# Pairing input spectra with adding transfers instead of pairing kernel spectra on VectorE, in a four-layer S4 and SwiGLU kernel

## The chip, the cores and the metric

The program runs on one core of a Trainium2 chip. The metric is device time in microseconds (us) of one execution, from outside the profile; the profile has its own, slightly shorter span from first to last instruction. Engines are named as in the profile: PE is TensorE (PEld its weight loads), DVE is VectorE, ACT is ScalarE, POOL is GpSimd, SP is SyncE, which here only issues DMAs.

## What is computed

The input is a sequence of 2048 rows of 512 channels. Two layers follow one another, each an S4 convolution and a SwiGLU feed-forward network (FFN), each behind a layer norm and with a residual:

```python
def _A_ref(u, A_re, A_im, B_re, B_im, C_re, C_im, log_dt, Dskip):
    ...
    P = jnp.exp(logdA[:, :, None] * l[None, None, :])
    K = jnp.einsum("dn,dnl,dn->dl", Cc, P, dB).real
    ...
    Yf = Uf * Kf[None, :, :, :]
    ...
    y = (lambda x, *d: x.transpose(*d))(y, 0, 2, 1) + u * Dskip[None, None, :]
    return y
...
x = x + _A_ref(_layernorm(x, axis=-1), A_A_re, A_A_im, A_B_re, A_B_im, A_C_re, A_C_im, A_log_dt, A_Dskip)
x = x + _B_ref(_layernorm(x, axis=-1), B_w_gate, B_w_up, B_w_down)
```

So per channel a kernel K of 2048 lags is built from 128 complex modes, the input is convolved with it causally, and the direct term u times Dskip is added. Both layers use the same parameters, so K is built once.

## The kernel before

**Blocks.** The sequence is cut into four blocks of 512 rows. A block of inputs and a block of lags are transformed by a discrete Fourier transform (DFT) of length 1024 at odd half frequencies, written as matmuls with cosine and sine tables (`ef`, `ek`), in four parts q and two halves h of 256 channels. An output block b is the inverse transform of the sum over k of (input spectrum of block b-k) times (spectrum W of lag block k). A product of two blocks of 512 spreads over 1024 outputs, so the second half of each product belongs to the next block. Before, this is put into the kernel spectra: W of block k is the transform of lag block k plus that of lag block k-1 with real and imaginary parts swapped and a sign, which shifts it by 512.

**Generation (to about 270 us).** K is built in eight chunks of 64 channels. Per chunk: `gen_turns` (DVE, angles as integer turns by doubling), `gen_trig` (ACT, sine and cosine) and `gen_exp` (ACT, exponentials) fill `re` and `im`, the large factor for lags that are multiples of 32; `gen_e` (DVE, L428 to L441) multiplies phase and size; `gen_g` (DVE, L443 to L476) builds `g`, the small factor for lags 0 to 31, by doubling. For the last doubling of chunks 1 to 6 one product is added by an accumulating DMA that POOL issues (L465). `lags` (L478) makes all lags of the 64 channels: per channel four small matmuls, two with `re` and two with `im` as the moving operand (f32 matmuls appear as two instructions), with the channels of a group of 16 on one of four 32-column strips of TensorE, so that four run beside each other. Before, `re` is laid out as 65 lags by 64 channels, so a matmul for one channel reads every 64th element. `spread_in` and `spread` (two DMA trips through DRAM) or `spread_pe` turn the lags into `kt`, and `spectra` (L526) transforms them: matmuls in `products` (L515) into PSUM tile `pw`, among them a matmul of one row that adds Dskip to all frequencies (L517), two ACT copies with a sign and swapped parts (L542), one ACT copy of block 0 into the resident `w0r` (L543), one DVE add (L545), and two stores into the DRAM array `wdr`. `later_parts` (L563) and `first_parts` (L551) do the same for the last two chunks, after the loop.

**Order in generation.** It is written out by hand: `manual_schedule` keeps program order on ACT, DVE and PE (and on SP inside the loop). Steps are put into a list `plan` with a due time each (`at(t, step)`, L986), chunk c starting at `starts[c]`, 28 units apart from chunk 3 on. The list is sorted and executed; the due times set only the order, the chip sets the pace. In the loop chunk i is in `use` (lags and spectra), chunk i+1 in `factors` (`gen_g`, `gen_e`), chunk i+2 in `prepare` (angles and exponentials). Between them run `second_block` (forward transform of input block 1 by `direct`, L283) and the sums of squares of the FFN weights (`norms`).

**The rest.** Eight pairs of (layer, block) follow in the order `SEQ` (L44). `ssm_half` (L716) computes a convolution: per q it loads W of block k and the older input spectra `uu` from DRAM (arrays `wdr`, `udr`), multiplies on DVE (L754), adds (L757), and transforms back (L773). The newest spectrum `u` comes from `forward` (L242; DVE butterflies, PE matmuls L273, ACT copy L275), one q ahead of its use, and is stored to `udr` by a POOL DMA (L706). `ffn` (L869) has the large matmuls (L886 to L903). Here the scheduler of the framework orders the engines, with a priority boost on some stretches. Tiles share a few buffers by tag: `uu` has three, `u` two, `w` three, `t1` three.

Of the kernel before, what the change touches and what calls it, by code (L numbers as in the profile page):

```python
# [22 lines left out]
P = 128  # L23
# [50 lines left out]
def kernel(ctx, tc, x, a_re, a_im, b_re, b_im, c_re, c_im, log_dt, d_skip,  # L74
# [65 lines left out]
    one = sb.tile([P, 1], F32, name="one")  # L140
    G.memset(one, 1.0)
# [4 lines left out]
    udr = [dram.tile([NB - 1, 2, 4, P, 2, HD], F32, name=f"udr{i}") for i in range(NL)]  # L146
    xdr = dram.tile([NB, 4, P, D], F32, name="xdr")
# [94 lines left out]
    def forward(n, h, eh):  # L242
# [13 lines left out]
        for i, q in enumerate(QORD):  # L256
# [4 lines left out]
            if eh:  # L261
                hl = z2[:, 1].bitcast(F16).rearrange("p i (l d) -> p l i d", l=2)
                A.activation(hl[:, 0], z, AF.Copy, scale=256.0)
                stt(hl[:, 1], z, 256.0, hl[:, 0], OP.subtract)
            pf = psml([P, 2, HD], "pf")
            with tc.high_priority(offset=BOOST):
# [7 lines left out]
                u = tl([P, 2, HD], "u", "u")  # L274
                A.activation(u, pf, AF.Copy, scale=2.0 ** -16 if eh else 1.0)  # L275
# [7 lines left out]
    def direct(b, h, q, n, space=psml):  # L283
# [9 lines left out]
        nc.sync.dma_start(udr[0][b, h, q], u)  # L293
# [58 lines left out]
    def gen_tiles(ch):  # L352
        re = tl([P, 65, DC], "re", f"W{2 * (ch % 2)}")
        im = tl([P, 65, DC], "im", f"W{2 * (ch % 2) + 1}")
        mu = tl([P, 32, DC], "mu", "n")
        xz = tl([P, 3, 5, DC], "xz", "bd")
        mz = mz2[:, ch % 2]
        return re, im, mu, xz, mz


# [14 lines left out]
    def gen_turns(ch, ts):  # L375

        re, im, mu, xz, mz = ts
# [3 lines left out]
        tu = im[:, 33:65].bitcast(I32)  # L381
# [3 lines left out]
        for n in (2, 4, 8, 16):  # L385
            V.tensor_tensor(tu[:, n:2 * n], tu[:, 0:n], tu[:, n - 1:n].to_broadcast([P, n, DC]), OP.add)
            yield
        G.memset(im[:, 32], 0.0)
        yield

    def gen_trig(ts):


        re, im, mu, xz, mz = ts
        A.activation(xz[:, 2], xz[:, 1].bitcast(I32), AF.Sin, scale=-TWO_PI / TURN)
        for c, s in ((xz[:, 0], xz[:, 1]), (re[:, 33:65], im[:, 33:65])):
            turns = s.bitcast(I32)
            A.activation(c, turns, AF.Abs)
            A.activation(s, turns, AF.Sin, scale=TWO_PI / TURN)
            A.activation(c, c, AF.Sin, scale=-TWO_PI / TURN, bias=hpi)  # L400
            yield

    def gen_exp(ch, ts):


        re, im, mu, xz, mz = ts
# [4 lines left out]
        G.memset(re[:, 0], 1.0)  # L411
        for a in sorted(LOW):
            A.activation(re[:, a], r_, AF.Exp, scale=32.0 * a)
# [3 lines left out]
    def upper(ts):  # L417

        A.activation(ts[2][:, 1:], ts[0][:, 1:32], AF.Square)

    def squares(ts):

        re = ts[0]
        for st in (2, 4):
            A.activation(re[:, st:33:2 * st], re[:, st // 2:17:st], AF.Square)
            yield

    def gen_e(ts):  # L428
# [3 lines left out]
        half = [[t.rearrange("p a (g h d) -> p a g h d", g=4, h=2)[:, :, :, o] for t in (re, mu)] for o in range(2)]  # L432
        V.tensor_tensor(im[:, :32], im[:, 64:32:-1], re[:, :32], OP.mult)
# [802 lines left out]
```

## Time and profile before

| what | value |
|---|---|
| time, median of 3 runs | 1186.87 us (1183.84 to 1190.97) |
| the profiled execution's own time | 1186.51 us |
| its span | 1184.7 us |
| instructions in the span | 24523 |
| ACT busy | 587.1 us (50%) |
| POOL busy | 92.2 us (8%) |
| moved by DMA | 151.17 MB, mean 128 GB/s |
| mean granted TensorE clock | 0.991 |

Busy times are unions over an engine's instructions. Matmuls are pipelined and last longer in the trace than they occupy the array, so a PE at 100% has no gap longer than a pipeline's depth, which does not by itself make it the limit. The profile's lists of groups give for each source line its engine, operation, shape, count, total busy time, mean ns of one, and the idle time of the engine just before with what ended it. The chain is followed back from the last instruction.

### The profile page before, as it was taken

The page shows a single profiled execution, that of the slowest core. Times are in us where ns is not written, and L with a number is a line of the kernel's source. Part 1 is how long each engine was busy: PE and PEld are TensorE (multiplying, and loading weights), DVE is VectorE, ACT ScalarE, POOL GpSimd, SP SyncE. Part 2 cuts the span into 40 slices and gives each one's busy share as a digit, 9 for nine tenths or more (in the row PEclk, how much of TensorE's full clock was granted, in tenths as well). Part 3 has the DMA queues.
Part 4 walks back from the last instruction along what each step waited for, and adds up shares of the span by engine and source line. Part 5 has one row for each costly group of instructions (what it writes and reads, how often), then busy time and mean ns, then how long its engine had stood idle before and what let it go on. Part 6 is the DMA issues. An engine that isn't in the chain of part 4 may idle for free.

```text
span 1184.7 us, 24523 instructions
## 1 busy us (share of the span) xinstructions
PE 1117.3 (94%) x10008; PEld 884.8 (75%) x10008; DVE 1006.2 (85%) x1591; ACT 587.1 (50%) x1180; POOL 92.2 (8%) x151
## 2 busy tenths in 40 slices
PE   1979999999789988999999999989999999999998
PEld 1868888888776857777778687858777686876875
DVE  7999999987789898999899999989994899983211
ACT  6677888833461554546654443655533452324211
POOL 1011111110000010002000000211000010000000
PEclk9989999999899999999999999999999999999999
DMA  6266666757484337432353354333544144312000
GB/s 231 91 162 149 162 166 162 182 179 240 125 271 140 115 119 200 118 96 84 92 152 128 112 165 155 96 104 115 149 116 165 46 121 130 118 49 45 14 24 18
DMA packets 136532, 151.17 MB, mean 128 GB/s; under 512 B 75474, under 2 KB 83666, under 8 KB 136419
## 3 DMA queue, kind: packets, MB, share of 16 engines
q1 hardware_dynamic: 129314, 126.47, 35.8%
q0 software_dynamic: 7104, 23.14, 7.3%
q8 instruction: 78, 1.28, 0.5%
q14 instruction: 36, 0.29, 0.1%
HBM read 101.85 MB, written 31.46 MB: 113 GB/s over the span
## 4 chain that ended last, share of the span: by engine, by line
PE 37%; DVE 27%; issue 4%; DMA 4%; ACT 2%; SPq 1%; POOL 0%; DVEq 0%; ACTq 0%; POOLq 0%
PE pgu L886 6%; PE pgu L887 6%; PE pgu L889 6%; DVE t L754 5%; DVE yk L757 5%; PE py L901 4%; PE py L902 3%; PE py L903 3%; PE pi L773 3%; PE pf L273 3%; DVE yk L754 2%; DVE z L229 2%; DVE sg L893 2%; DMA mix<-nn 1%; DVE bb L229 1%
## 5 line engine op out<-in xcount | busy, mean ns | idle before, releaser
L886 PE MATMUL pgu<-mix,wsl 128*128 128x256 f16 x1280 | 299.7, 273 | 6.9 <-DVE sg L893 4.4
L887 PE MATMUL pgu<-mix,wsl 128*128 128x256 f16 x1280 | 299.7, 273 | 0.0
L889 PE MATMUL pgu<-mix,wsl 128*128 128x256 f16 x1280 | 195.6, 273 | 0.0
L887 PEld LDWEIGHTS <-wsl 128*128 128x128 f16 x1280 | 125.5, 98 | 24.3 <-issue 8.0
L901 PE MATMUL py<-wsl,hh 128*128 128x512 f16 (+1 forms) x352 | 134.2, 381 | 8.6 <-DVE xg L906 6.9
L886 PEld LDWEIGHTS <-wsl 128*128 128x128 f16 x1280 | 125.4, 98 | 16.0
L889 PEld LDWEIGHTS <-wsl 128*128 128x128 f16 x1280 | 125.5, 98 | 14.9
L903 PE MATMUL py<-wsl,hl 128*128 128x512 f16 (+1 forms) x352 | 134.1, 381 | 0.2 <-DVE hl L895 0.2
L902 PE MATMUL py<-wsl,hh 128*128 128x512 f16 x320 | 121.8, 381 | 0.0
L754 DVE TENSOR_TENSOR t<-uu,w 128x1024 f32<-128x1024 f32 x96 | 116.9, 1218 | 2.6 <-DMA w<-wdr 2.4
L757 DVE TENSOR_TENSOR yk<-yk,t 128x1024 f32<-128x1024 f32 x96 | 116.9, 1217 | 0.3
L892 ACT ACTIVATE sg<-pgu,sc 128x512 f32<-128x512 f32 x80 | 54.6, 683 | 121.0 <-PE pgu L889 115.9
L893 DVE SCALAR_TENSOR_TENSOR sg<-pgu,sc,sg 128x512 f32<-128x512 f32 x80 | 59.6, 745 | 56.6 <-ACT sg L892 56.5
L515 PE MATMUL pw<-kt,ek 128*128 128x256 f32 (+1 forms) x384 | 94.1, 382 | 0.0
L894 ACT ACTIVATE hh<-sg 128x512 f16<-128x512 f32 x80 | 50.0, 626 | 76.1 <-DVE sg L893 76.0
L773 PE MATMUL pi<-yl,mix 128*128 128x256 f16 x576 | 78.9, 273 | 5.0 <-DVE yl L229 2.7
L515 PEld LDWEIGHTS pw<-kt,ek 128*128 128x128 f32 x384 | 70.8, 194 | 8.9
L273 PE MATMUL pf<-z,eh 128*128 128x256 f16 x576 | 74.9, 273 | 0.0
L754 DVE TENSOR_TENSOR yk<-u,w0r 128x1024 f32<-128x1024 f32 x56 | 68.2, 1218 | 1.5 <-ACT u L275 1.5
L902 PEld LDWEIGHTS <-hh 128*128 128x128 f16 (+1 forms) x352 | 34.6, 98 | 46.1 <-issue 10.6
L895 DVE TENSOR_TENSOR hl<-sg,hh 128x512 f16<-128x512 f32 x80 | 54.8, 686 | 15.6 <-ACT hh L894 15.5
L485 PE MATMUL pk<-re,g 128*32 128x64 f32 x1024 | 65.0, 317 | 2.8 <-DVE re L440 2.8
(239 smaller groups left out, 2154.3 us busy)
## 6 DMA issues: line engine op xcount, KB each, us to landing
w<-wdr SPq DMA_DIRECT2D x96, 256.0 KB, 2.7
uu<-udr SPq DMA_DIRECT2D x96, 256.0 KB, 3.0
udr<-u POOLq DMA_DIRECT2D x32, 256.0 KB, 2.7
g<-acc POOLq DMA_DIRECT2D x6, 1024.0 KB, 8.4
udr<-u SPq DMA_DIRECT2D x16, 256.0 KB, 2.1
n<-ndr SPq DMA_DIRECT2D x16, 256.0 KB, 3.9
n<-xdr SPq DMA_DIRECT2D x4, 1024.0 KB, 5.7
kdr<-ks SPq DMA_DIRECT2D x6, 512.0 KB, 2.7
```

The costliest lines, as they stand in the source:

```text
L273: PE.matmul(pf[:, o], lhsT=e, rhs=m, start=k == 0, stop=k == len(terms) - 1)
L515: PE.matmul(pw[:, i], lhsT=e, rhs=kt[:, :, c + 4 * k0:4 * k1:4, :].rearrange("p g k d -> p k g d"), start=c == 0, stop=c == 3)
L754: V.tensor_tensor(t, uu.unsqueeze(1).to_broadcast([P, 2, 2, HD]), w.unsqueeze(2).to_broadcast([P, 2, 2, HD]), OP.mult)
L757: V.tensor_tensor(yk, yk, t, OP.add)
L773: PE.matmul(pi[:, o], lhsT=e, rhs=m, start=k == 0, stop=k == len(terms) - 1)
L886: PE.matmul(o, lhsT=wgu(wi, k, 0)[:, fs], rhs=nh[:, k], start=k == 0, stop=False)
L887: PE.matmul(o, lhsT=wgu(wi, k, 1)[:, fs], rhs=nh[:, k], start=False, stop=False)
L889: PE.matmul(o, lhsT=wgu(wi, k, 0)[:, fs], rhs=nlo[:, k], start=False, stop=k == 3)
L893: V.scalar_tensor_tensor(sg, pgu[:, 1], sc6[:, 4:5], sg, OP.mult, OP.mult)
L901: PE.matmul(py[:, r], lhsT=hh[:n, f, rc], rhs=wd(f, 0)[:n], start=f == 0, stop=False)
L902: PE.matmul(py[:, r], lhsT=hh[:n, f, rc], rhs=wd(f, 1)[:n], start=False, stop=False)
L903: PE.matmul(py[:, r], lhsT=hl[:n, f, rc], rhs=wd(f, 0)[:n], start=False, stop=f == FT - 1)
```

## The change

It has three parts.

1. **Pairing moves from kernel to input.** W of block k is now the plain transform of lag block k, and the input spectrum carries the swapped one of the block before. `spectra` and `later_parts` copy `pw` straight to SBUF in one ACT instruction; the DVE add is gone. Each new input spectrum is computed into `own`; a new helper `carry` writes it, parts swapped and one negated (one ACT instruction, two SP stores), to DRAM (`pdr`, or for block 0 straight into `udr` of block 1). The next block's spectrum loads it into `u` (SP) and adds `own` by an accumulating POOL DMA. In `ssm_half` the products run from the oldest input to the newest.
2. **Layout of the large factor.** `re`, `im` and `mu` are laid out as 16 groups of (lags by 4 channels). A matmul for one channel now reads every fourth element. The angles are built in a tile of their own, 16 lags at a time, so `gen_trig` works in two halves with one DVE step between them; the scalar_tensor_tensor of `gen_e` becomes four, one per channel of a group of four, each with a step of four elements; other instructions keep their number of elements.
3. **Direct term.** The one-row matmuls are gone; `skip` adds Dskip to lag 0 of `kt` on DVE (one partition, 64 elements) ahead of the matmuls.

The due times of `prepare` follow the new steps, and the last step of `gen_g` moves behind one more entry. Cut to its core:

```diff
     def forward(n, layer, b, h, eh):
...
+            u = own = tl([P, 2, HD], "u", "u")
+            if b:
+                nc.sync.dma_start(u, pdr[layer][b - 1, h, q])
+                own = tl([P, 2, HD], "own", "uu")
...
-                u = tl([P, 2, HD], "u", "u")
-                A.activation(u, pf, AF.Copy, scale=2.0 ** -16 if eh else 1.0)
+                A.activation(own, pf, AF.Copy, scale=2.0 ** -16 if eh else 1.0)
+            if b:
+                G.dma_start(u, own, accum_op=OP.add)
+            if b < NB - 1:
+                carry(pdr[layer][b, h, q], q, own)
+                G.dma_start(udr[layer][b, h, q], u)
             yield q, u
...
-        nc.sync.dma_start(udr[0][b, h, q], u)
+        if b:
+            G.dma_start(udr[0][b, h, q], u, accum_op=OP.add)
+        else:
+            nc.sync.dma_start(udr[0][b, h, q], u)
+        carry(udr[0][1, h, q] if b == 0 else pdr[0][b, h, q], q, u)
...
+        re = tl([P, DC // 4, 65, 4], "re", f"W{2 * (ch % 2)}")
+        im = tl([P, DC // 4, 65, 4], "im", f"W{2 * (ch % 2) + 1}")
+        mu = tl([P, DC // 4, 32, 4], "mu", "n")
...
+        t16 = tl([P, 16, DC], "t16", "z")
...
-        for n in (2, 4, 8, 16):
+        for n in (2, 4, 8):
             V.tensor_tensor(tu[:, n:2 * n], tu[:, 0:n], tu[:, n - 1:n].to_broadcast([P, n, DC]), OP.add)
             yield
+        V.tensor_tensor(tu, tu, tu[:, 15:16].to_broadcast([P, 16, DC]), OP.add)
...
+        for m in (33, 49):
+            circle(re[:, :, m:m + 16], im[:, :, m:m + 16], t16)
+            if m == 49:
+                cosine(re[:, :, 33:65])
             yield
...
-        V.scalar_tensor_tensor(im[:, 33:64], im[:, 31:0:-1], -1.0, mu[:, 1:], OP.mult, OP.mult)
+        for e in range(4):
+            V.scalar_tensor_tensor(im[:, :, 33:64, e], im[:, :, 31:0:-1, e], -1.0, mu[:, :, 1:, e], OP.mult, OP.mult)
...
             if n == 16 and 0 < ch < NCH - 1:
+                yield
                 tmp = tl([P, 2, 16, DC], "acc", ("gb", "ga")[ch % 2])
...
+                PE.matmul(pd, lhsT=f, rhs=z[:, d // 4, 0:64, e], start=i == 0, stop=i == 1, tile_position=(0, 32 * grp))
...
+    def skip(ch, kt):
+
+        k = kt[0:1, :, 0]
+        V.tensor_tensor(k, k, dsk[:, ch * DC:(ch + 1) * DC].rearrange("p (g d) -> p g d", g=4), OP.add)
...
-            if (i, c) == (0, 0) and k0 == 0:
-                PE.matmul(pw[:, 0, 0], lhsT=one[0:1].to_broadcast([1, P]), rhs=dsk[:, ch * DC:(ch + 1) * DC], start=False, stop=False)
...
+    def carry(o, q, u):
+
+        n = 1 - q % 2
+        t = tl([P, HD], "neg", "t1")
+        A.activation(t, u[:, n], AF.Copy, scale=-1.0)
+        nc.sync.dma_start(o[:, 1 - n], t)
+        nc.sync.dma_start(o[:, n], u[:, 1 - n])
...
-        for i, sign in signs(q0):
-            A.activation(wv[:, :, i], pv[:, :, 1 - i, :3 * DC], AF.Copy, scale=sign)
+        A.activation(wv, pv[:, :, :, DC:], AF.Copy)
         A.activation(w0r[:, h, q0::2, :, off:off + DC], wf[:, :, :, 0], AF.Copy)
         yield
-        V.tensor_tensor(wv, pv[:, :, :, DC:], wv, OP.add)
-        yield
...
-            for i, sign in signs(q):
-                A.activation(wo[:, i, 0], w0[:, 1 - i], AF.Copy, scale=sign)
-                A.activation(wo[:, i, 1:], pw[:, 1 - i, :2], AF.Copy, scale=sign)
-            V.tensor_tensor(wo, pw, wo, OP.add)
+            A.activation(wo, pw, AF.Copy)
...
-            for k in range(b + 1):
+            for k in range(b, -1, -1):
...
-            at(t + 13.0, steps["turns"], 6)
-            at(t + 17.0, tr, 2)
-            at(t + 8.3, steps["exp"], 100)
+            at(t + 0.35, steps["turns"])
+            at(t + 0.45, tr)
+            at(t + 6.9, steps["turns"], 4)
+            at(t + 7.2, tr)
+            at(t + 11.25, steps["turns"])
+            at(t + 11.3, tr)
+            at(t + 11.35, steps["exp"], 100)
...
+            at(t + 17.1, lambda: skip(c, kt))
```

108 lines of the change are left out of this document (55 added, 53 removed).

## The prediction

> **What bounds the kernel now.** I read the page first, then busy time by stretches, cut where the lags of a chunk begin, then a stretch of the timeline, the groups by shape, and the waits.
>
> ```profile
> span 1184.7 us, 24523 instructions
> PE 1117.3 (94%) x10008; PEld 884.8 (75%) x10008; DVE 1006.2 (85%) x1591; ACT 587.1 (50%) x1180; POOL 92.2 (8%) x151
> ```
>
> Two engines are nearly full over the whole span, so the stages decide. Busy time by stretches (stretch, length, then PE, PEld, DVE, ACT, POOL busy, granted clock, DMA share, GB/s):
>
> ```profile
> 62.00:89.30 27.30, 22.71 (x284) 17.98 (x277) 26.86 (x33) 20.98 (x46) 4.91 (x9) 0.90 0.63 160
> 119.15:148.01 28.86, 28.86 (x351) 24.55 (x350) 28.41 (x36) 23.87 (x54) 4.76 (x9) 1.00 0.66 166
> 176.79:205.50 28.71, 28.71 (x350) 24.45 (x349) 27.10 (x32) 23.44 (x54) 4.17 (x8) 1.00 0.64 160
> 234.42:265.70 31.28, 31.28 (x387) 25.71 (x386) 26.42 (x29) 12.28 (x24) 3.27 (x6) 1.00 0.61 187
> 265.70:345.00 79.30, 70.10 (x672) 63.10 (x672) 63.41 (x117) 40.30 (x78) 2.30 (x2) 0.96 0.64 205
> 410.00:1110.00 700.00, 681.92 (x5731) 527.58 (x5730) 625.10 (x1040) 321.08 (x621) 51.70 (x64) 1.00 0.39 115
> ```
>
> The reader is to see three things. Until 89 us DVE alone is full. In the five periods from 89 to 234 us, of which two are shown, PE has no gap and DVE works about 27.8 of 28.8 us: both must get shorter before the period does. The last period is PE's. From 410 us on PE is busy 97% of the time; nothing in the change takes PE or DVE work out of that stretch. So the gain can come only from the 177 us between 89 and 266 us and a little behind them, and the long rest can only lose.
>
> **PE in a period.** The timeline at the end of one chunk's lags and the start of its spectra:
>
> ```profile
> 148.01 0.49 PE L485 MATMUL pk<-re,g 128*32 128x64 f32 x8
> 148.54 0.51 PE L485 MATMUL pk<-re,g 128*32 128x64 f32 x8
> 155.97 0.47 PE L486 MATMUL pk<-im,g 128*32 128x64 f32 x8
> 156.37 0.70 PE L515 MATMUL pw<-kt,ef 128*128 128x256 f32 x2
> 157.00 0.43 PE L517 MATMUL pw<-tdk,one 1*128 1x64 f32 x2
> 157.35 1.56 PE L515 MATMUL pw<-kt,ek 128*128 128x256 f32 x6
> 158.75 0.59 PE L515 MATMUL pw<-kt,ef 128*128 128x256 f32 x2
> 275.97 1.93 PE L507 MATMUL kp<-ks,ident 128*32 128x256 f32 x32
> ```
>
> With the one-row matmul between, the six matmuls of the next line start 157.35 - 156.37 = 0.98 us after the first pair; those six take 158.75 - 157.35 = 1.40 us, so two take 0.47. L517 costs the other 0.51 us, four times in a period: **-2.0 us of PE per period**, 28.8 to 26.8.
>
> The lags: sixteen matmuls start every 148.54 - 148.01 = 0.53 us, that is 0.13 us for four on the four strips, 2.0 ns for each of the 64 columns. L507 also uses four strips, but its moving operand is contiguous: 32 matmuls of 256 columns in 1.93 us, whose last one ends some 0.38 us after its start, leave 1.55 us for seven steps, 0.22 us per four, 0.9 ns per column. The lags' operand has a step of 64 elements, which looks like the reason for 2.0. What a step of four elements costs no row shows. Bounds: nothing gained (2.0 ns stays) to 64 x 1.1 ns x 64 steps = 4.5 us per period. I take nothing: below 26.8 us of PE, DVE is the limit anyway.
>
> **DVE in a period.** Groups by shape (count | busy, mean ns | idle before):
>
> ```profile
> L545 DVE TENSOR_TENSOR spare<-pw,spare 128x768 f32<-128x768 f32 x6 | 5.7, 952 | 1.3 <-ACT w0r L543 1.3
> L437 DVE SCALAR_TENSOR_TENSOR im<-im,mu 128x1984 f32<-128x1984 f32 x6 | 13.3, 2219 | 0.0
> L472 DVE TENSOR_TENSOR spare<-g,xz 128x512 f32<-128x512 f32 x6 | 4.1, 688 | 0.0
> L454 DVE TENSOR_TENSOR g<-g,spare 128x64 f32<-128x64 f32 x5 | 1.1, 226 | 0.0
> L485 PEld LDWEIGHTS pk<-re,g 128*32 128x32 f32 x711 | 35.2, 157 | 1.9 <-issue 1.9
> L507 PEld LDWEIGHTS kp<-ks,ident 128*32 128x32 f32 x32 | 0.9, 110 | 0.8 <-issue 0.3
> ```
>
> Two pair adds go: -1.9 us. `skip` comes: 0.2 us by L454 (64 elements; fewer partitions save nothing that a row shows, at worst it waits for the kt transfers, but it stands just ahead of the matmuls that already wait for them). The scalar_tensor_tensor of 1984 elements becomes four of 496: 4 x 0.68 (L472, 512 elements) = 2.7 instead of 2.2, **+0.5 us** if a step of four elements costs DVE nothing. No row of DVE has such a step. Lower bound: 4 x 0.43 by pipelining as in the present 2.2, about 0; upper: every element at the 2.0 ns that the lags' stepped columns take on PE, 4 x (0.99 + 0.16) = 4.6 us, **+2.4**. I take +0.5, the nearest rows on the same engine. Angles and the other products keep their element counts. Sum: 27.8 - 1.9 + 0.2 + 0.5 = 26.6 of DVE work; about half of its present 1 us of gaps stays, 27.2. So the period falls from 28.8 to **27.2 us, -1.6**.
>
> The Trainium skill speaks against part 2 here: "SBUF — State Buffer", section "Specifications (TRN2)", gives SBUF lines of 16 bytes, of which an access pattern must hit each at least twice for full bandwidth, with a penalty for each change of line. A step of four f32 elements changes line every time, by which the new layout would gain PE nothing and would slow the four stepped instructions; a note in the same page's section "Door 1: The DMA port swizzle" says the opposite, that a step of up to four f32 is free. The trace agrees only so far as a step of 64 is slow (2.0 against 0.9 ns; weight loads of 32 columns 157 against 110 ns). The result by the strict reading is the third rival below.
>
> **ACT and POOL in a period.** ACT loses a little in `spectra`, gains two extra starts of the halved angles, 0.4 us for `carry` (128x256), and a wait for the DVE step between the halves. That DVE step in turn waits until ACT has read the first half; by the due times ACT reads it at 7.2 and DVE comes at 11.25, after most of `gen_g`, and behind it on DVE stands the last product of `gen_g` (L464). At 23.4 to 23.9 of 28.8 us it has room for 3 us of that. `gen_exp` queues behind the waiting instruction, but its result is used only in the next period. At nothing, then; if the room were gone, ACT would hold the period near 27. The factor's accumulating transfer is tighter:
>
> ```profile
> 161.32 2.29 DVE L464 TENSOR_TENSOR acc<-g,xz 128x2048 f32<-128x2048 f32 x1
> 163.91 1.24 POOL L465 DMA_DIRECT2D g<-acc  x1 [3.93 <-DVE acc L464]
> 167.33 0.95 DVE L545 TENSOR_TENSOR spare<-pw,spare 128x768 f32<-128x768 f32 x1
> 175.80 0.28 DVE L451 TENSOR_TENSOR g<-w,re 128x128 f32<-128x128 f32 x1
> g<-acc POOLq DMA_DIRECT2D x6, 1024.0 KB, 8.4
> ```
>
> It lands about 163.9 + 8.4 = 172.3; L451, the first write into its source buffer, comes at 175.8, 3.5 us later. Between the two DVE did the angle steps (163.5 to 166.9), which now come earlier, and a pair add, which goes; 0.7 us come in. The margin falls to about zero. I count no wait, and keep it as a rival.
>
> **Generation, summed.** The start and the first period (to 89 us, DVE full, no pair add yet) take 0.5 + 0.7 = +1.2. Five periods: 5 x -1.6 = -8.0. The last, PE's: -2.0. Behind it (265.7 to 345 us) go four more one-row matmuls (L560, about 0.5 us each) and, in six units, a DVE add and three ACT instructions each; PE and DVE have gaps there, so I count -1.5. Sum: **-10.3 us**.
>
> **The rest.** Per new spectrum with an older block, 40 of them: a 256 KB load on SP, an accumulate on POOL, and for 32 one ACT copy and two SP stores.
>
> ```profile
> udr<-u POOLq DMA_DIRECT2D x32, 256.0 KB, 2.7
> L706 POOL DMA_DIRECT2D udr<-u x32: 539/542/607, 410.9 to 886.4; - x32
> DVE yk L754 <- ACT u L275: 1.5, 1, 1.5
> 716.63 0.60 ACT L275 ACTIVATE u<-pf 128x512 f32<-128x512 f32 x1 [4.04 <-PE pf L273]
> 718.35 1.22 DVE L754 TENSOR_TENSOR yk<-u,w0r 128x1024 f32<-128x1024 f32 x1
> 806.03 0.60 ACT L275 ACTIVATE u<-pf 128x512 f32<-128x512 f32 x1 [1.09 <-PE pf L273]
> 818.90 1.22 DVE L754 TENSOR_TENSOR yk<-u,w0r 128x1024 f32<-128x1024 f32 x1
> SPq L750 <- DVE t L754: 129.8, 37, 9.4
> ```
>
> The accumulate lies between a plain 256 KB store (0.5 issue + 2.7) and the 1 MB accumulate (1.2 + 8.4): 3.2 to 9.6 us; I take 5, nearer the row of its size. Before, u was ready 12.3 us ahead of its use in the second pair shown and 1.1 us in the first; DVE waited for it once. Such short margins are few (first q of a block), and the new order uses u last, after at least one more product and add (2.4 us) for each older block. So 5 us are mostly covered. Uncovered remain 1 to 3 us in one or two places; POOL's store of u now waits for the accumulate and holds back the norm's `pow` behind it; SP, whose loads already stand waiting for buffers (last row), gets 104 more DMAs, with loads of W and the FFN's transposes behind them. `own` takes a `uu` buffer, which shortens the prefetch. PE's work covers most: **+2**, between 0 and +21 (third paragraph below).
>
> **Forecast.** 1186.5 - 10.3 + 2 = **1178 us**, against the profiled execution's own 1186.51, which is 0.4 below the median of 1186.87. Its own range is 1173 to 1183.
>
> **Rivals.**
> 1. *The stepped reads get fast.* If a step of four is free on PE, the lags drop by up to 4.5 us; in five periods DVE's 26.6 binds (its gaps close: another -2), in the last PE's gain counts in full (-4): 1172. For it: 0.9 ns in L507. Against: no row with such a step.
> 2. *The factor's accumulate takes the place of the pair add.* If POOL has three weight loads ahead of it (0.56 us each, 1.7 together), L451 waits 1.7 us a period and 27.2 is 28.9 again: five times -1.6 become five times 0.1 and -10.3 shrinks to -2: with the rest's +2 it is 1186, no change. It decides once the issue slips by more than the zero margin.
> 3. *The stepped instructions are slow on DVE (slower).* +2.4 instead of +0.5 makes DVE's period 29.1: 5 x 0.3 + 5.2 at the start (two chunks at 2.4 + 0.2) - 2.0 - 1.5 + 2 = +5: 1191. The point from which it decides is a mean of about 1.1 us for one of the four.
> 4. *The input comes late (slower).* If the small accumulate costs the 9.6 us of the large one, each of the 40 inputs whose margin is below it stalls DVE by the difference: I estimate some 12 of them (the first of a block, as in the first pair above, and most of block 1 of layer 1, with one older block to hide behind) by 2 us on average, +24, of which PE hides few: -10 + 21 = +11: 1197. It decides where 9.6 exceeds margin plus 2.4 us per older block.
>
> **How the numbers follow.** Chances: forecast 0.48, rivals 0.15, 0.12, 0.10, 0.15. A measurement of this kernel tells about 0.5%, 5.9 us, from no change: faster is below 1181, slower above 1192.8. Faster: 0.42 of the forecast's 0.48 and rival 1, 0.57. Same: the forecast's rest, rival 2 and half of 3, 0.23. Slower: half of 3, 4: 0.20. Low end 1167, a little under rival 1; high end 1198, at rival 4; about 0.15 lies outside.
>
> **What would show it.** Right: lags of successive chunks start 27 us apart, DVE full and PE with gaps; L517 and L545 gone; stepped instructions at 0.68 us; DVE waits for u under 5 us in all. Wrong: a mean near 1.15 us (rival 3); L451 waiting for the factor's transfer (2); DVE or PE waiting for u, or the FFN's transposes queued on SP, for more than 10 us after 410 (4); lags' four under 0.09 us (1).

## The result and the profile after

The changed kernel takes **1410.6 us** (median of 4 runs, 1409.7 to 1416.9) against 1187.1 for the kernel before: a ratio of **1.189, 95% interval 1.184 to 1.194**. The forecast was 1178, with a range up to 1198. The profiled execution is the longest of the four, 6 us above the median.

The page of the changed kernel: the span, the engines, and from the 40 slices PE's busy tenths and the granted clock. Below it are the same two rows of the kernel before.

```profile
span 1415.1 us, 24824 instructions
PE 1159.5 (82%) x9948; PEld 901.8 (64%) x9948; DVE 1021.9 (72%) x1604; ACT 603.3 (43%) x1214; POOL 125.9 (9%) x198
PE   2768788798889889958999994799889828993698
PEclk9989899899999899999999997899999958996799
```

```profile
PE   1979999999789988999999999989999999999998
PEclk9989999999899999999999999999999999999999
```

No engine has much more work than before: PE 1159.5 instead of 1117.3 us, DVE 1021.9 instead of 1006.2. The span is 230 us longer, so most of the loss is waiting. PE's row has holes (4, 2, 3 tenths) in the second stage, the part behind the generation, where it had none, and the clock falls in the same slices (7, 5, 6 tenths). PE is busy 42 us longer for 60 matmuls fewer, which bounds what slower matmuls can have added; the rest of the loss has to be in what PE waits for.

Busy time by stretches, cut at the start of a chunk's lags as before, and the second stage from 410 to 1110 us (length, then PE, PEld, DVE, ACT, POOL busy, granted clock, DMA share, GB/s):

```profile
104.20:138.03 33.83, 29.15 (x346) 24.60 (x350) 18.77 (x16) 24.51 (x54) 5.71 (x10) 0.90 0.62 153
138.03:176.12 38.09, 28.31 (x346) 24.22 (x350) 37.44 (x55) 24.03 (x54) 5.71 (x10) 0.87 0.56 132
176.12:209.43 33.31, 28.67 (x345) 24.60 (x349) 27.16 (x35) 23.54 (x53) 5.17 (x9) 0.90 0.60 146
281.08:309.86 28.78, 28.78 (x381) 24.59 (x385) 17.12 (x15) 12.07 (x21) 4.11 (x7) 1.00 0.57 162
410.00:1110.00 700.00, 615.84 (x4925) 465.26 (x4922) 524.41 (x877) 277.77 (x551) 65.69 (x89) 0.94 0.47 132
```

Periods are 33 to 38 us, not 27. PE fills none of the first three. DVE fills the second (37.4 of 38.1 us), after standing idle for almost half of the first: the two periods together hold 56 us of DVE in 72. The last period shown is PE's, as before, and fell from 31.3 to 28.8 us. The last chunk's lags start at 309.9 us instead of 265.7: **+44 us in the generation**. What follows them is 1105 us long instead of 919: **+186 us behind it**. In its 700 us PE works 616 instead of 682.

One period of the changed kernel, ACT and PE by their timeline (start, us, engine, line; in brackets the idle time before and who ended it):

```profile
184.25 1.02 ACT L526 ACTIVATE ks<-pk 128x1024 f32<-128x1024 f32 x1 [2.12 <-PE pk L516]
186.12 1.05 ACT L417 ACTIVATE im<-t 128x1024 f32<-128x1024 int32 x1
188.46 1.06 ACT L416 ACTIVATE re<-t 128x1024 f32<-128x1024 int32 x1 [0.16 <-DVE t L406]
194.40 3.01 ACT L441 ACTIVATE re<-rho 128x64 f32<-128x64 f32 x20
199.24 0.87 ACT L334 ACTIVATE sq<-st 128x344 bf16<-128x344 f32 x2
```

```profile
187.20 1.23 DVE L406 CUSTOM_DVE_ANT_0 t<-t 128x2048 uint16<-128x2048 uint16 x1 [4.96 <-ACT im L417]
199.78 0.82 PE L337 MATMUL nrm<-sq,onesb 128*128 128x344 bf16 x2 [4.64 <-ACT sq L334]
```

Three engines wait for one another in turn. The first half of the angles (L417) stands on ACT behind the copy of the lags, which waits for PE; DVE's last angle step waits 5 us for it; ACT's second half waits for DVE, and the exponentials (L441) stand behind that half; the squares (L334) stand behind those, and PE's sum of squares, with the matmuls of the next spectra queued behind it, waits 4.6 us.

In the second stage, the chain that ended last around one block's start, and four of the rows of SP's waits after 410 us (queue and line, what ended the wait, us in total, times, longest; L558 is a store of `carry`, L776 loads W, L778 loads `uu`):

```profile
1146.62 0.60 ACT own L277
1147.52 3.56 DMA u<-own
1151.14 2.61 DMA uu<-udr
1153.79 1.87 DVE bt L228 x6
```

```profile
SPq L558 <- ACT own L277: 116.8, 19, 11.2
SPq L778 <- DMA u<-own: 51.2, 9, 9.1
SPq L776 <- DVE t L780: 48.8, 29, 5.1
SPq L778 <- DVE yk L780: 21.5, 7, 10.5
```

The load of an older spectrum (`uu`, L778) starts when an accumulate that has nothing to do with it lands (1147.52 + 3.56): the accumulate reads `own`, and `own` held the buffer that the load needs, since the three buffers of `uu` are used in turn, as a ring. The sums of SP's waits are no prices: before, its loads already waited 129.8 us for DVE.

### The profile page after: what moved, and what is told of

Its sections match the earlier page's. It is cut to its first block, busy times and chain, and to the rows that moved or that the text cites. A ratio compares the mean times of both kernels' runs of the same rounds, so it can differ in the third digit from the quotient of the medians.

```text
span 1415.1 us, 24824 instructions
## 1 busy us (share of the span) xinstructions
PE 1159.5 (82%) x9948; PEld 901.8 (64%) x9948; DVE 1021.9 (72%) x1604; ACT 603.3 (43%) x1214; POOL 125.9 (9%) x198
## 4 chain that ended last, share of the span: by engine, by line
PE 43%; DVE 22%; issue 13%; DMA 9%; ACT 9%; SPq 2%; POOL 1%; DVEq 0%; ACTq 0%; POOLq 0%
PE pgu L912 7%; PE pgu L915 7%; PE pgu L913 7%; DMA uu<-udr 4%; PE pf L276 4%; PE pi L799 3%; PE py L927 3%; PE py L929 3%; PE py L928 3%; DVE t L780 3%; PE pw L550 3%; DMA mix<-nn 2%; PE pk L516 2%; DVE yk L783 2%; DVE yk L780 2%
## 5 line engine op out<-in xcount | busy, mean ns | idle before, releaser
L799 PE MATMUL pi<-yl,mix 128*128 128x256 f16 x576 | 92.7, 299 | 93.7 <-ACT yl L788 83.7
L276 PEld LDWEIGHTS <-eh 128*128 128x128 f16 x576 | 61.1, 106 | 81.2 <-issue 67.8
L276 PE MATMUL pf<-z,eh 128*128 128x256 f16 x576 | 89.8, 297 | 6.5 <-DVE z L228 4.6
L799 PEld LDWEIGHTS <-mix 128*128 128x128 f16 x576 | 61.1, 106 | 51.8 <-issue 38.5
L550 PEld LDWEIGHTS pw<-kt,ek 128*128 128x128 f32 x384 | 77.1, 205 | 10.3
L780 DVE TENSOR_TENSOR yk<-uu,w 128x1024 f32<-128x1024 f32 x48 | 58.4, 1218 | 29.6 <-DMA uu<-udr 25.4
L788 ACT ACTIVATE yl<-mix,sy 128x512 f16<-128x512 f32 x48 | 34.5, 719 | 99.0 <-DVE mix L785 98.8
L228 DVE SCALAR_TENSOR_TENSOR z<-z 128x512 f16<-128x512 f32 x48 | 33.0, 688 | 54.7 <-ACT z L262 46.8
```

What stands on the lines that cost most here:

```text
L276: PE.matmul(pf[:, o], lhsT=e, rhs=m, start=k == 0, stop=k == len(terms) - 1)
L550: PE.matmul(pw[:, i], lhsT=e, rhs=kt[:, :, c + 4 * k0:4 * k1:4, :].rearrange("p g k d -> p k g d"), start=c == 0, stop=c == 3)
L780: V.tensor_tensor(t, uu.unsqueeze(1).to_broadcast([P, 2, 2, HD]), w.unsqueeze(2).to_broadcast([P, 2, 2, HD]), OP.mult)
L799: PE.matmul(pi[:, o], lhsT=e, rhs=m, start=k == 0, stop=k == len(terms) - 1)
```

## The experiments

The first theory was that the parts are separable: the layout costs the generation, the pairing costs the rest. Runs given without an interval are single executions; repeated executions of one kernel lay up to 12 us apart (wacc_direct, 1199.7 to 1211.2). Code is cut to what matters. Each part alone:

**layout** keeps the second part of the change only, with its due times.

> Only the layout of the large factor in runs of four channels, with the two-part angles and the generation's new due times; the spectra are still paired by VectorE and the direct term is still the one-row matmul. Theory A: the parts add up, and the layout alone gives the generation's loss (the changed kernel's lags end 44 us later, at 318.1 instead of 273.6) and none of the rest's, so 1187 + 44 = about 1231 us (1220 to 1240), with lags again up to 38 us apart. Theory B: the generation's loss comes with the pairing (accumulates on POOL, wider copies on ACT), so the layout alone stays within 1180 to 1195 us.

Measured: 1252.7 us, ratio 1.055 (1.052 to 1.058). The lags' starts are 38 to 41 us apart in six periods, the last start at 330 us, 64.6 later than before; the rest is as long as before. That is theory A's shape, but 13 us above its range: the generation alone loses 65 us, not the 44 of the whole.

**pairing** keeps the first part only.

> Only the pairing moved to the input spectra (carry, accumulates, order of the products); layout and direct term as before. Theory A: the two VectorE adds leave the generation (952 ns each, 1.9 us a period) and the rest pays the 186 us that the changed kernel lost after its lags, so about 1187 + 186 = 1373, less up to 13 us of generation: 1355 to 1380 us. Theory B: the whole loss of 224 us is the pairing's, about 1410 us. Theory C: the rest's loss needs the generation's late end or the lower granted clock (0.914 against 0.991) that comes with it: below 1300 us.

Measured: 1362.4 us, 1.148 (1.145 to 1.151). The last lags start 1.5 us later than before, so the pair adds that left VectorE gained nothing there, and the rest is 172 us longer.

**direct** keeps the third part only.

> Only the direct term: VectorE adds it to lag 0 (one row add a chunk) and the one-row matmuls of 0.51 us are gone, 4 a period and 12 in the first parts. Theory A (TensorE holds the period, as the prediction had it): 2.0 us less in each of 7 periods, less where VectorE holds it, and up to 6 us in the first parts, so 1170 to 1182 us. Theory B (VectorE or the handshakes hold the period): within 0.5% of 1187 us.

Measured: 1183.05 us, **0.997 (0.995 to 0.998)**. Two of its periods:

```profile
148.89:176.14 27.25, 25.44 (x341) 22.54 (x341) 26.63 (x33) 21.84 (x50) 4.25 (x8) 0.94 0.67 161
176.14:204.30 28.16, 26.73 (x343) 23.59 (x341) 27.71 (x35) 23.21 (x53) 4.25 (x8) 1.00 0.65 163
```

PE's work fell by the 2 us that were reckoned, or a little more, and in these two, among the three shortest, DVE, 26.6 of 27.3 and 27.7 of 28.2, took over as the limit. The seven periods are 27.2 to 30.7 us long, against 28.6 to 31.3 before. The gain is 4 us, which lies in theory B's range.

The three parts alone cost 65.8, 175.5 and -3.9 us, 237 together, against 223.5 for the whole. So the parts nearly add up, as theory A has it. They do so partly by luck: in the profiles the generation loses 65 us by the layout alone and 44 in the whole, while the rest loses 172 by the pairing alone and 186 in the whole. Theory B of the first two runs falls. Theory C of the pairing falls for the late end of the generation (the pairing alone has none); the lower clock came with the pairing alone too (0.932), so this run doesn't part the two. With the buffer of its own below, the clock is 0.979.

### The generation

In the layout alone, DVE and ACT by their timeline:

```profile
159.02 1.22 DVE L395 CUSTOM_DVE_ANT_0 t<-t 128x2048 uint16<-128x2048 uint16 x1
160.15 2.28 DVE L483 TENSOR_TENSOR acc<-g,xz 128x2048 f32<-128x2048 f32 x1
171.25 0.96 DVE L564 TENSOR_TENSOR spare<-pw,spare 128x768 f32<-128x768 f32 x1 [8.82 <-ACT w0r L562]
```

```profile
160.27 1.06 ACT L405 ACTIVATE re<-t 128x1024 f32<-128x1024 int32 x1 [3.20 <-DVE t L395]
166.21 3.01 ACT L430 ACTIVATE re<-rho 128x64 f32<-128x64 f32 x20
170.10 0.85 ACT L561 ACTIVATE spare<-pw 128x384 f32<-128x384 f32 x2
```

Between DVE's last angle step and the pair add that waits for L561 and L562, ACT has 11 us of work (160.3 to 171.2), sines, exponentials and the two copies, and DVE 2.3. Theory O: it is this place in ACT's order. Theory S, the rival: it is what the steps of four cost VectorE. **layout_due** gives chunks 2 to 5 of the layout alone the order of before, and their last angle step a buffer `tv` of its own, as it now runs before ACT has read `tu`:

```diff
             at(t + 0.05, tiles)
...
+            if c < 6:
+                at(t + 13.0, steps["turns"], 6)
+                at(t + 17.0, tr, 3)
+                at(t + 8.3, steps["exp"], 100)
+                return
             at(t + 0.35, steps["turns"])
...
-        V.tensor_tensor(tu, tu, tu[:, 15:16].to_broadcast([P, 16, DC]), OP.add)
+        V.tensor_tensor(tv, tu, tu[:, 15:16].to_broadcast([P, 16, DC]), OP.add)
```

> The layout alone (1252 us), with the due times of before for the angles, the trigonometry and the exponentials of chunks 2 to 5 (exponentials ahead of the angles' second half, the trigonometry at the end of the period), and a second angle buffer for these chunks in memory that is free at that time. Theory O (ACT's block of trigonometry and exponentials, 11 us, behind VectorE's last angle step and ahead of the copies that VectorE waits for, makes the period): four periods of 38 to 40 us fall to 29 to 31, so 1210 to 1222 us. Theory S (the stepped operations cost VectorE the time): the periods stay above 36 us and the time above 1240.

Measured: 1215.5 us. Two mended periods and the first of the two that keep the change's due times:

```profile
122.68:152.51 29.83, 28.69 (x351) 24.32 (x351) 29.38 (x36) 24.66 (x60) 4.83 (x9) 1.00 0.69 171
152.51:182.74 30.23, 28.52 (x350) 24.20 (x350) 29.78 (x37) 23.36 (x55) 4.24 (x8) 1.00 0.65 158
182.74:224.32 41.58, 31.45 (x349) 25.77 (x349) 32.39 (x41) 21.04 (x50) 4.23 (x8) 0.84 0.51 127
```

In one kernel, with the same work in each period, 30 us with the old due times and 42 with the new: theory O. The second buffer takes a wait away only where there is one; the layout alone has none of DVE for ACT's reading of the angles between its second and its last lags. What is left over the 28.8 of before is now DVE's, 29.4 of 29.8.

**layout_tt** takes the stepped instructions out of the layout alone:

```diff
-        for e in range(4):
-            V.scalar_tensor_tensor(im[:, :, 33:64, e], im[:, :, 31:0:-1, e], -1.0, mu[:, :, 1:, e], OP.mult, OP.mult)
+        V.tensor_tensor(im[:, :, 33:64], im[:, :, 31:0:-1], mu[:, :, 1:], OP.mult)
```

> The layout alone, with the four stepped scalar_tensor_tensor operations of a chunk (1065 ns each) replaced by one tensor_tensor over all four channels of the runs, which leaves out the minus sign of that part of the large factor. Theory S: about 2 us of VectorE less in each of 8 chunks and all of it on the path, 15 us or more: 1237 us or less. Theory O: VectorE has 9 us of idle time in a period behind ACT, so what it saves is mostly waited: 1240 to 1253 us.

Measured: 1245.5 us, 7 less than the layout alone, and periods that stay at 38 to 41 us. Theory S is a small part of it.

### The second stage

**pair_noacc**, the pairing alone without the accumulate:

```diff
-            if b:
-                nc.sync.dma_start(u, pdr[layer][b - 1, h, q])
-                own = tl([P, 2, HD], "own", "uu")
...
-            if b:
-                G.dma_start(u, own, accum_op=OP.add)
```

> The pairing alone, but in the second stage nothing is added to an input spectrum: the load of the carry and the accumulate are left out (the products of blocks after the first in the second stage so lack the paired part), and the spectrum goes to u and to the store as before; the negated copies on ACT and the carry stores on SP's queue stay. Theory C1: the accumulate with what waits for it (POOL's store, the norm's power behind that, the product that waits for u) is the loss, so 1175 to 1200 us. Theory C2: the carry stores that wait for ACT at the head of SP's queue are the loss, so above 1300 us. Between the two both count.

Measured: 1195.2 us. It looked like theory C1, but the edit takes away three things: the accumulate, the load, and `own` as a tile of `uu`. The next three part them.

**pair_store** stores the block's own spectrum before the accumulate is issued, so that POOL's store waits for none:

```diff
-            if b:
-                G.dma_start(u, own, accum_op=OP.add)
             if b < NB - 1:
                 carry(pdr[layer][b, h, q], q, own)
-                G.dma_start(udr[layer][b, h, q], u)
+                G.dma_start(udr[layer][b, h, q], own)
+            if b:
+                G.dma_start(u, own, accum_op=OP.add)
```

> The pairing alone, but POOL stores the block's own spectrum before it issues the accumulate, so that no store waits for an accumulate and the norm's power isn't held behind one (the later products of older blocks so lack the paired part). Theory P (POOL's wait, 79 us in 22 waits for u<-own in the pairing alone): below 1290 us. Theory U: own still stands in the ring of uu, so 1335 to 1365 us.

Measured: 1366.8 us, nothing gained: POOL's wait (theory P) costs nothing.

**pair_ownbuf**, with every transfer and wait of the pairing kept:

```diff
-    BUFS = dict(W0=1, W1=1, W2=1, W3=1, ga=1, gb=1, n=1, bt=1, z=1, u=2, y1=1, uu=3, w=3, t=1, bd=2, t1=3,
+    BUFS = dict(W0=1, W1=1, W2=1, W3=1, ga=1, gb=1, n=1, bt=1, z=1, u=2, y1=1, uu=2, w=3, ow=1, t=1, bd=2, t1=3,
...
-                own = tl([P, 2, HD], "own", "uu")
+                own = tl([P, 2, HD], "own", "ow")
```

> The pairing alone (1362 us), with all its transfers and waits, but the tile of the block's own spectrum no longer takes its turn among the three buffers of uu: uu has two, and own has one of its own, so the memory is the same. Theory U (own, held until the accumulate and the carry store have read it, stands in the ring of the uu loads, and the order written for TensorE then leaves the spectra behind the end of the feed-forward work): near the run without accumulates, 1185 to 1215 us. Theory C1 (the serial 4.6 us of the accumulate, POOL's wait for it, the late u): still above 1320 us.

Measured: **1219.6 us**, 1.025 (1.021 to 1.030): 143 of the pairing's 175 us are gone with one buffer's name. The same 700 us of the second stage, first in the pairing alone, then with the own buffer:

```profile
410.00:1110.00 700.00, 589.82 (x4673) 442.61 (x4672) 528.08 (x878) 277.45 (x555) 70.79 (x92) 0.92 0.48 135
```

```profile
410.00:1110.00 700.00, 659.73 (x5475) 509.38 (x5473) 620.66 (x1029) 320.00 (x635) 80.62 (x102) 0.98 0.56 156
```

DVE gets back 93 us of work in the same time. Two of SP's waits, again first in the pairing alone, then with the own buffer:

```profile
SPq L538 <- ACT own L279: 92.7, 18, 9.6
SPq L760 <- DMA u<-own: 42.9, 9, 10.3
```

```profile
SPq L538 <- ACT own L279: 31.2, 11, 13.6
SPq L760 <- DVE yk L762: 25.9, 24, 3.9
```

The wait of the load of `uu` for an accumulate is no longer in the list; what is left is one of the load of `u` (33.6 us in two waits). The order of the instructions changed with it. In the pairing alone 360 of TensorE's matmuls for the input spectra and the inverse transforms stand in four groups of 48 to 144 between the last matmul of one feed-forward network and the first of the next, 41 to 49 us apart, where PE has nothing else to do. In the kernel before and with the own buffer no such group has more than 13 matmuls or lasts longer than 2 us.

**pair_dve** asks whether the accumulate is needed for this. VectorE adds the carry, `own` stays in the ring:

```diff
...
-                A.activation(own, pf, AF.Copy, scale=2.0 ** -16 if eh else 1.0)
-            if b:
-                G.dma_start(u, own, accum_op=OP.add)
+                if b < NB - 1:
+                    A.activation(own, pf, AF.Copy, scale=2.0 ** -16 if eh else 1.0)
+                if b:
+                    stt(u, pf, 2.0 ** -16 if eh else 1.0, u, OP.add)
```

> The pairing alone with VectorE adding the carry, so that nothing accumulates in the second stage, but own in the ring of three uu buffers; the same with own in a buffer of its own took 1210 us. Theory U1 (any tile of another rhythm in the ring is the cause, here held until the carry stores have read it): above 1260 us. Theory U2 (only the accumulate's time in the ring is the cause): 1205 to 1225 us.

Measured: 1277.6 us, and **ownbuf_dve**, the same with the own buffer, 1210.5:

> The pairing alone with own in its own buffer (1219.6 us), but VectorE adds the loaded carry to the spectrum out of the accumulator's memory, 30 operations over 512 elements of about 0.7 us, and no transfer accumulates in the second stage. Theory D2 or P2 (the accumulate's serial time is what is left): 32 us less and 21 us of VectorE more where it is the bound, 1200 to 1212 us. If the carry's loads and stores on SP's queue are what is left: 1220 to 1240 us.

So the ring costs 67 us without any accumulate in it, and 143 with one. Theory U1. In SP's waits the rows are, for pair_dve, this one, and with the own buffer the largest on `own` is 18.3 us:

```profile
SPq L539 <- ACT own L280: 71.0, 13, 11.5
```

What of the pairing's cost is left beside the buffer? **ownbuf_store** makes the edit of pair_store with the own buffer, **before_uu2** takes the third `uu` buffer from the kernel before:

> The pairing alone with own in its own buffer (1219.6 us), and POOL stores the block's own spectrum before it issues the accumulate (the later products of older blocks so lack the paired part). Theory P2 (what is left of the pairing's cost, 32 us, is POOL's wait for the accumulate): 1187 to 1205 us. Theory D2 (it is VectorE's: the product that waits for the accumulated u, and the added loads): 1210 to 1225 us.

> The kernel before, with two buffers of uu instead of three and nothing else. If the 32 us that the pairing with its own buffer still costs are the third buffer's: 1205 to 1220 us. If they are the accumulate, the added loads and stores: 1184 to 1192 us.

Measured: 1221.2 us, no gain, so POOL's wait is free here too; and 1194.4 against 1188.6 (where executions of the kernel before reach 1192.4), so the lost buffer is about 6 of the 32 us. In ownbuf_dve VectorE's adds are 40, not the 30 I wrote, of 682 ns each, 27 us, and the kernel is 23 over before: there VectorE's own work would be enough to explain the rest, which isn't shown. How the 26 us of pair_ownbuf beyond the buffer divide between the accumulates and the added loads isn't settled.

### The whole change, mended

**after_own** is the whole change with the own buffer, **after_mended** with the own buffer and the edit of layout_due.

> The whole change (1410.6 us) with own in a buffer of its own beside two of uu, and nothing else. If the buffer gives back here what it gave in the pairing alone (1362 to 1220, 143 us): 1260 to 1275 us, with lags that end at about 318 us as in the change. If the generation's late end adds to the second stage: above 1285 us.

> The whole change (1410.6 us) with the two mends together: own in a buffer of its own beside two of uu, and the due times of before for angles, trigonometry and exponentials of chunks 2 to 5 with a second angle buffer. If the two causes are the whole loss and add up: four periods at the 27.2 us that the prediction reckoned (or 28.5 with what VectorE pays for the steps), two unmended at 33 to 38, the rest as with the own buffer alone (32 us over before): 1205 to 1235 us. If a cause is missing: above 1260 us.

Measured: 1269.3 us, so the buffer is 141 of the change's 223; and 1239.7 us, 1.043 (1.042 to 1.045). Its four mended periods are 29.6, 29.2, 30.2 and 26.7 us long, the two others 39.9 and 37.9. The second cause gives 30 us in four of six periods. What is left over the kernel before is 52 us: about the pairing's 32 with its own buffer, and 20 for the two unmended periods. So no further cause of size is needed, though 1240 lies above the range for the sum, by 5 us. The forecast's gain of 1.6 us a period isn't there even so: the four mended periods are 115.7 us together, against 116.0 before.

### The engines' account, and versions to beat the kernel before

**ownbuf_dve_direct** relieves PE and DVE in the generation without the layout:

> Pairing of the input spectra with own in its own buffer and VectorE's add of the carry (1210.5 us), with the direct term on VectorE too; the layout is that of before. In the generation TensorE has 26.1 us of work a period (the direct term's run) and VectorE 28.1 - 1.9 = 26.2. Theory G (these two engines set the period): about 27 us a period, lags ending near 262 instead of 276.6, and 1193 to 1200 us. Theory H (something else holds the period near 28.8): 1206 to 1211 us.

Measured: 1208.05 us, 1.016 (1.014 to 1.019); the last lags start at 261.6 instead of 265.7. Two of its periods:

```profile
150.46:176.84 26.38, 25.74 (x341) 22.62 (x341) 25.93 (x32) 21.85 (x50) 4.40 (x9) 0.94 0.79 184
176.84:204.62 27.78, 26.58 (x342) 23.65 (x342) 26.98 (x34) 24.23 (x53) 5.09 (x9) 1.00 0.70 175
```

With the next, of 27.9 us, these are about the 27 us of the prediction, in three of seven periods; the first three stay at 29 to 30. The gain of about 4 us in the generation doesn't pay for the second stage. The time itself came out as theory H.

Both of the next two have the direct term on VectorE and leave the second stage alone. **wacc_direct** pairs the kernel spectra by accumulating transfers; **pool_direct2** adds them on GpSimd (`wn` is a copy that ACT makes):

```diff
...
-        V.tensor_tensor(wv, pv[:, :, :, DC:], wv, OP.add)
-        yield
         for j in range(2):
             store_w(h, off, q0 + 2 * j, wo[:, j])
         yield
+        for j in range(2):
+            G.dma_start(wdr[1:, h, q0 + 2 * j, :, :, off:off + DC].rearrange("k p i d -> p i k d"),
+                        wn[:, j].rearrange("p i k g d -> p i k (g d)"), accum_op=OP.add)
```

> Kernel before with the direct term on VectorE, and the kernel spectra still paired, but by accumulating transfers into the stored spectra, outside the second stage: ACT writes both halves (0.8 us more a spectrum), POOL issues two accumulates a spectrum, VectorE's two adds of 0.95 us a period are gone. If TensorE and VectorE hold the period together, as the prediction had it, periods fall from 28.8 to about 27 and the time to 1170 to 1178 us. If ACT or the POOL queue (the factor's accumulate) takes over, 1180 to 1195 us, no better than the direct term alone (1183).

```diff
...
-        V.tensor_tensor(wv, pv[:, :, :, DC:], wv, OP.add)
+        G.tensor_tensor(wo, wo, wn, OP.add)
```

> The direct term on VectorE (1183 us), and the kernel spectra paired as before but added by GpSimd from two copies that ACT makes out of the accumulators (0.8 us more of ACT a spectrum); nothing changes in the second stage. Theory G: periods of about 27 us and 1168 to 1176 us. Theory H: 1180 to 1186 us. If GpSimd's adds are long enough to delay the factor's accumulate on its queue, or slow VectorE's operations beside them: 1186 us or more.

Measured: 1206.0 us, 1.015 (1.013 to 1.018), and 1200.4 us, 1.010 (1.008 to 1.011). One period's stretch of wacc_direct, the issues of its two accumulates, then six of GpSimd's 13 adds in pool_direct2, and one of the others with the VectorE instruction beside it:

```profile
148.00:177.00 29.00, 23.52 (x331) 20.33 (x330) 24.58 (x31) 23.96 (x55) 7.57 (x10) 0.94 1.02 189
```

```profile
g<-acc POOLq DMA_DIRECT2D x6, 1024.0 KB, 9.7
wdr<-wn POOLq DMA_DIRECT2D x26, 192.0 KB, 7.6
```

```profile
L548 POOL TENSOR_TENSOR spare<-spare,wn 128x768 f32<-128x768 f32 x6 | 18.2, 3039 | 27.9 <-issue 21.2 <-ACT spare L545 6.7
```

```profile
121.95 2.54 POOL L548 TENSOR_TENSOR wo<-wo,wn 128x768 f32<-128x768 f32 x1 [8.48 <-issue]
122.52 2.05 DVE L452 TENSOR_TENSOR g<-g,spare 128x64 f32<-128x64 f32 x1
```

In the one the 16 DMA engines are full (1.02) with pieces of 64 elements, and ACT waits 28.6 us for the accumulates to have read its copies; that this is the whole loss isn't shown. In the other GpSimd takes 2.6 to 3.0 us on average (medians 2.1 and 2.3) for what VectorE does in 0.95, and VectorE loses time beside it: the add of 64 elements shown takes 2.05 us, where its median without GpSimd (direct) is 0.22. Eleven VectorE instructions beside the 13 adds take 1.5 to 2.6 us longer than their median in direct, 20 us together, and the kernel is 17 us slower than direct: the expectation's last case. The direct term alone, at 0.997, is the only version here that beats the kernel before.

## Why the prediction was wrong

**What bounds the kernel.** PE and DVE as joint limits of a period held: each of the two, relieved alone, handed over to the other (pairing: nothing gained; direct: 4 us), and both relieved gave 26.4 to 27.9 us in three of seven periods. "The long rest can only lose" held too, at nine times the upper end that I gave it.

**The terms of the sum.** PE's -2.0 for the one-row matmul is right, and the last period, PE's, gained 2.5. The lags' bounds: sixteen matmuls still take 0.51 us on PE, so a step of four elements is as slow as one of 64, and "nothing" was the right choice. That the step is what makes them slow isn't shown, since no run has these columns contiguous.

```profile
209.34 0.47 PE L516 MATMUL pk<-re,g 128*32 128x64 f32 x8
209.60 0.46 PE L516 MATMUL pk<-im,g 128*32 128x64 f32 x8
209.85 0.44 PE L516 MATMUL pk<-re,g 128*32 128x64 f32 x6
```

The stepped scalar_tensor_tensor was mis-sized: 1058 ns against 680, close to rival 3's bound (four instructions a chunk, eight chunks).

```profile
L465 DVE SCALAR_TENSOR_TENSOR im<-im,mu 128x496 f32<-128x496 f32 x32 | 31.8, 1058 | 0.0
L468 DVE TENSOR_TENSOR re<-re,mu 128x992 f32<-128x992 f32 x16 | 18.3, 1182 | 0.0
```

That is 2.1 ns per element with single elements at a step of four, and 1.2 in the row below it, which reads tiles of the same layout in whole runs of four. It costs 2.0 us a chunk (4 x 1.06 - 2.22) instead of 0.5, and VectorE's full periods in layout_due, 30 us instead of 28.8, are where it shows. It also takes the forecast's gain: in the second and third period of after_mended VectorE has 28.3 and 28.7 us of work, not the 26.6 of the sum.

By the Trainium skill, "SBUF — State Buffer", section "Specifications (TRN2)", a line of 16 bytes must be hit at least twice for full bandwidth; these two rows and the lags agree with it, and not with the note in the same page's section "Door 1: The DMA port swizzle" that a step of up to four f32 is free.

**ACT "at nothing".** This step failed, for the +44 us. I compared due times (ACT reads at 7.2, DVE comes at 11.25) and ACT's busy share, 23.5 of 28.8 us. But due times set only an order. In that order the first half of the angles stands behind the lags' copy, the second half behind DVE, and 11 us of ACT's work behind that, ahead of what DVE and PE wait for next. I named `gen_exp` as queued behind the waiting instruction and looked at who uses its result; who stands behind `gen_exp` was the question. The price by layout_due is about 10 us a period in the layout alone; in the whole change periods of 33 to 38 us against the mended 29 make it 4 to 9, perhaps because VectorE has no pair add left there that waits (43.7 us of waits for ACT in the layout alone).

**The rest, "+2".** This step failed, for the +186. The accumulate itself was sized a little high. Its row (KB of each, median us from issue to landing):

```profile
u<-own POOLq DMA_DIRECT2D x40, 256.0 KB, 3.7
```

I took 5 us. (The bounds of 3.2 and 9.6 added the issue's own time to a landing time that already holds it; by the rows they are 2.7 and 8.4.) And POOL's wait for it costs nothing (pair_store, ownbuf_store). What I put down as "`own` takes a `uu` buffer, which shortens the prefetch" is 141 us. It isn't a shorter prefetch (before_uu2 has that, for 6 us): `own` is written by ACT late, and read by the accumulate and by a store that waits its turn on SP, so its place in the ring comes free in another rhythm than that of a loaded spectrum. That path is read from the waits; the runs show only that the shared buffer is the cause. Loads and carry stores stand in one queue on SP; a load there waits for the readers of `own` (51.2 us in the changed kernel), a store for `own` itself (116.8), and everything behind waits with them. DVE, which had 625 us of work in 700, has little room to make up such gaps. The order of the instructions has the same cause: feed-forward matmuls stand ahead of the spectra until there are none left. That order is the scheduler's, and the only thing that differs for it between pairing and pair_ownbuf is the buffer. How much the chip would have lost with the ring shared and the old order was not tried, since the buffer changes both.

**The rivals.** Rival 4 had the stage and neither the mechanism nor the size: the accumulate doesn't cost 9.6 us, and DVE waits 0.3 us after 410 us for a fresh u, under 5 as the forecast had it. What it waits for there are late transfers of SP's queue, the transposes that the sign of rival 4 named (25.9 us in the whole execution, 4.0 before) and older spectra (25.4, none to speak of before):

```profile
DVE nn L865 <- DMA mix<-nn: 25.9, 10, 4.3
DVE yk L780 <- DMA uu<-udr: 25.4, 9, 5.1
```

Rival 3 had the mechanism and 2.0 of its 2.4 us, but it is not what decided. Rivals 1 and 2 didn't occur in the changed kernel: no row of DVE's waits there is on the factor's transfer.

**The range.** It had the buffer and ACT's order within "+2, between 0 and +21" and "at nothing". Both were waits whose place I had named and priced without following the queue to its end.

## What to carry to other kernels

A tile that joins a shared ring of buffers can hold the next load until its slowest reader is done, and with it all that stands behind that load on an in-order queue; here the scheduler's order got worse with it. Give a tile with another life a buffer of its own, even if the ring gets shorter (143 us for one, against about 6 for the lost buffer). A step that is split between two in-order engines is priced by what stands behind each half in both orders, not by busy shares. Of two engines that bound a stage together, relieving one is worth what the other leaves.

## What the runs showed of the hardware beyond that

An accumulating transfer of 256 KB between SBUF tiles in rows of 2 KB lands 3.7 us after its issue, little over the 2.7 to 2.9 of a plain store of that size to DRAM; one of 192 KB into DRAM in pieces of 256 bytes takes 7.6 us, against 3.7 for the plain store of that shape in the same run (wacc_direct). GpSimd's add of 768 elements a partition takes 2.1 to 2.3 us in the median and 2.6 to 3.0 on average, and a VectorE instruction beside it can take 1.5 to 2.6 us longer than alone (pool_direct2). The granted clock falls where PE has holes (layout_due: 0.84 in the 42 us period, 1.00 in the 30 us ones beside it).
